# Four adjacent rows of w_v on a partition, and the columns of w_k cast into the same order

## The chip, the cores and the metric

The kernel runs on one core of a Trainium2 chip. The metric is the device time of one execution in microseconds (us). The engines are named as in the profile: PE is TensorE's matmul (PEld its weight load), DVE is VectorE, ACT is ScalarE, POOL is GpSimd, and SP is SyncE, which here only issues transfers (DMAs). "L638" is line 638 of the kernel.

## What is computed

Attention with a sliding window of 128 and 4 sink keys, over q, k, v of shape (4, 8, 768, 64), gives x of shape (4, 768, 512). Behind it comes a channel mix:

```python
x_prev = concatenate([zeros((B, 1, D)), x[:, :-1, :]], axis=1)
xk = mu_k * x + (1.0 - mu_k) * x_prev
xr = mu_r * x + (1.0 - mu_r) * x_prev
k = maximum(xk @ w_k, 0.0)                 # w_k: 512 x 1024
v = k * k @ w_v                            # w_v: 1024 x 512
r = 1.0 / (1.0 + exp(-(xr @ w_r)))         # w_r: 512 x 512
return r * v
```

The 1024 columns of w_k are the 1024 rows of w_v: the hidden index f. A sum over f does not depend on the order in which f is taken, as long as k and w_v agree on it.

## The kernel before, in words

The work is cut into 12 units of 256 rows: 4 batches of 3 tiles. Each unit passes through four functions. `prepare` casts q, k and v to bf16 and transposes q and k. `attend` makes the scores of the heads (PE, L812), their exponentials (ACT, L884), the mask product (DVE, L898), the values (PE, L917) and the scaled x (L935 or L944). `mix` transposes x and makes xk and xr (DVE, L998 and L1009). `ffn` makes relu(xk @ w_k) in chunks of 128 hidden columns with the chunk on the partitions (PE, L1062; relu at L1072 or L1076; squares at L1085 or L1089), the gate (PE, L1101; tanh at L1107), then the product with w_v (PE, L1119, in two parts of four chunks each), and last the gated output (DVE, L1128) and its store (L1135).

**Order.** Every operation is entered with `P.op`: its engine, its cost in ns, what it reads, writes, takes and holds. The order on each engine is written out by hand in `ORDER`, and the engine of the operations that could run on several in `CHOICE`. `Plan.schedule` goes through these orders with the costs, gives out buffers of the pools, and puts filler products (`fill`, L1141) into PE's order where its own clock says that PE stands idle in the first 40 us. So a cost changes neither order nor engine, but can change which buffer of a pool an operation gets and which filler stands where.

**Weights.** `load_weight` (L486) loads them in fp32 into three buffers of one pool, `w32`, each 128 partitions x 4 x 512 numbers, 1 MB. The loads come in the order w_k first half, w_k second half, w_r, w_v first half, w_v second half, all on SP's queue. The buffers of w_k are used again for w_v, so a w_v load waits for the casts of the w_k half in its buffer. A load of w_v puts row 128c + p on partition p, for four values of c: four pieces of 2 KB a partition. A load of a w_k half takes 512 columns of row 128c + p, also four pieces of 2 KB.

**Casts.** `cast` (L626) turns a quarter of a weight to bf16, 1024 numbers a partition. The four casts of w_k are operations 79 to 82: ACT (columns 0 to 255), POOL (256 to 511), ACT (512 to 767) and DVE (768 to 1023). Those of w_v are 85 to 88: DVE, DVE, ACT, DVE; they also multiply by 0.5. PE's first `ffn` takes the hidden chunks in the order 0, 2, 1, 3, then 6, 7, then 4, 5, so that it waits for ACT's first cast, POOL's, DVE's and ACT's second in that order. The product at L1119 waits with its first part for the first two casts of w_v, and with its second part for the last two, ACT's and DVE's.

Of the kernel before, what the change touches and what calls it, by code (L numbers as in the profile page):

```python
# [11 lines left out]
AF = mybir.ActivationFunctionType  # L12
# [345 lines left out]
def kernel(  # L358
# [14 lines left out]
    nc = tc.nc  # L373
# [14 lines left out]
    P = Plan()  # L388
# [25 lines left out]
    buf = P.buf  # L414
# [5 lines left out]
    def dve(n, rate=1.04):  # L420
        return 69.0 + rate * n

    def act(n):
        return 67.0 + 0.833 * n
# [61 lines left out]
    def load_weight(what, rank):  # L486
        name, part = what[:2], what[2:]
        src = {"wk": moe_w_k, "wr": moe_w_r, "wv": moe_w_v}[name].rearrange(
            "(c p) f -> p c f", p=128)
        i = "ab".index(part) if part else 0  # L490
        if name == "wk":
            src = src[:, :, 512 * i:512 * i + 512]
        elif name == "wv":
            src = src[:, 4 * i:4 * i + 4]
        key = ("w32", name, i)
        P.op("SP", 600.0, lambda: nc.sync.dma_start(out=buf[key], in_=src), rank,
             service=2930.0, descs=660, take=[("w32", key)], writes=[(name + "32", i)])

    for i, what in enumerate(LOADS):
        if what[0] == "w":  # L500
            load_weight(what, i - 100)
        elif what == "kq0":
            load(0, "kq", -100, 0, 4)
            load(0, "kq", -99.5, 4, 8)
        else:
            load(int(what[-1]), what[:-1], i - 100)
# [7 lines left out]
    for i, src in enumerate((moe_mu_k, moe_mu_r)):  # L514
        P.op("ACT", 500.0, lambda i=i, src=src: nc.scalar.dma_start(
            out=rows8[NC * i:NC * i + NC, :], in_=src.rearrange("(c p) -> c p", p=128)), -100,
            writes=[("mu8", i)], service=40.0, descs=4)
# [98 lines left out]
    def spread_mu():  # L616
# [5 lines left out]
         hold=["mup"], reads=["mup"], writes=[("mu", 0), ("mu", 1)])  # L622
# [3 lines left out]
    def cast(out, name, i, cut, rank, writes):  # L626
        key = ("w32", name, i)
        half = name == "wv"

        def emit(by):  # L630
            if by == "ACT":
                return lambda: nc.scalar.activation(out=out, in_=buf[key][cut], func=AF.Copy,  # L632
                                                    scale=0.5 if half else 1.0)
            engine = nc.vector if by == "DVE" else nc.gpsimd
            if half:
                return lambda: nc.vector.tensor_scalar(out=out, in0=buf[key][cut], scalar1=0.5,
                                                       scalar2=None, op0=ALU.mult)
            return lambda: engine.tensor_copy(out=out, in_=buf[key][cut])  # L638

        P.op("DVE", dve(1024, 0.52), emit("DVE"), rank, port=True, hold=[key],  # L640
             alts={"DVE": (dve(1024, 0.52), emit("DVE"), True),
                   "ACT": (act(1024) + 30.0, emit("ACT"), False)} |
             ({} if half else {"POOL": (1100.0, emit("POOL"), True)}),
             reads=[(name + "32", i)], writes=writes)

    for i in range(4):
        j = i % 2
        cast(wk_sb[:, :, 256 * i:256 * i + 256], "wk", i // 2,
             (slice(None), slice(None), slice(256 * j, 256 * j + 256)), 2 + i, [("wk", i)])
    for i in range(2):  # L650
        cut = (slice(None), slice(2 * i, 2 * i + 2))
        cast(wr_sb[cut], "wr", 0, cut, 8 + i, [("wr", i)])
    for i in range(4):
        j = i % 2
        cast(wv_h[:, 2 * i:2 * i + 2, :], "wv", i // 2,
             (slice(None), slice(2 * j, 2 * j + 2)), 11 + i, [("wv", i)])
# [546 lines left out]
```

## Time and profile before

| what | value |
|---|---|
| timed runs | 167.26, 169.18 and 169.84 us, median 169.18 |
| the profiled execution's own time | 166.92 us |
| its span (first to last instruction) | 165.1 us |
| busy: PE, DVE, ACT, POOL | 155.0, 144.8, 136.9, 35.2 us |
| granted clock of PE | 1.00 |
| loads of w_k, from issue to landing (median of two) | 10.3 us |
| loads of w_v, from issue to landing (median of two) | 11.2 us |
| casts of w_k: ACT (two), POOL, DVE | 1.06 (mean), 1.47, 0.68 us |
| casts of w_v: DVE (three), ACT | 0.69 (mean), 1.06 us |

All durations come from one profiled execution. In a timeline row stand the start, the time that the group covers, the engine, the line, the operation, what it writes and reads, and how many instructions; in brackets the idle time of the engine just before, and what ended it. In the chain of waits each row is a piece of the chain that ended last: start, length, engine or transfer. Rows of groups by shape give, after the bar, the busy time in us and the mean ns of one instruction. "SPq" is the time that SP spends issuing a transfer, with the stops that a full queue makes.

### The profile page before, as it was taken

The page shows a single profiled execution, that of the slowest core. Times are in us where ns is not written, and L with a number is a line of the kernel's source. Part 1 is how long each engine was busy: PE and PEld are TensorE (multiplying, and loading weights), DVE is VectorE, ACT ScalarE, POOL GpSimd, SP SyncE. Part 2 cuts the span into 40 slices and gives each one's busy share as a digit, 9 for nine tenths or more (in the row PEclk, how much of TensorE's full clock was granted, in tenths as well). Part 3 has the DMA queues.
Part 4 walks back from the last instruction along what each step waited for, and adds up shares of the span by engine and source line. Part 5 has one row for each costly group of instructions (what it writes and reads, how often), then busy time and mean ns, then how long its engine had stood idle before and what let it go on. Part 6 is the DMA issues. An engine that isn't in the chain of part 4 may idle for free.

```text
span 165.1 us, 4735 instructions
## 1 busy us (share of the span) xinstructions
PE 155.0 (94%) x1840; PEld 102.3 (62%) x1862; DVE 144.8 (88%) x356; ACT 136.9 (83%) x249; POOL 35.2 (21%) x65
## 2 busy tenths in 40 slices
PE   7889889989999998998999999999999999999992
PEld 3446566656668676676566686575855764776541
DVE  7189999999999899999999999999889899777621
ACT  3698999988999999899989999999794898482440
POOL 2885311203621044033402412310010000000000
PEclk9999999999999999999999999999999999999999
DMA  4999989999798999999999998989995992401113
GB/s 138 252 351 354 298 230 338 382 388 312 200 321 196 180 302 252 173 196 267 176 219 172 240 126 200 227 176 125 208 208 87 233 212 78 191 4 64 64 74 117
DMA packets 74453, 34.38 MB, mean 208 GB/s; under 512 B 63800, under 2 KB 66112, under 8 KB 74432
## 3 DMA queue, kind: packets, MB, share of 16 engines
q1 hardware_dynamic: 74272, 34.02, 87.6%
q8 instruction: 14, 0.23, 0.6%
q14 instruction: 7, 0.06, 0.2%
q10 hardware_dynamic: 160, 0.07, 0.1%
HBM read 24.12 MB, written 6.29 MB: 184 GB/s over the span
## 4 chain that ended last, share of the span: by engine, by line
PE 64%; DVE 18%; DMA 10%; issue 3%; ACT 2%; SPq 1%; DVEq 0%
PE bank L1119 20%; PE bank L1062 19%; PE bank L1101 10%; DMA w<-in_moe_w_v_dram 7%; DVE e L898 6%; PE bank L917 4%; PE sc L812 4%; DMA vs<-in_v_dram 3%; DVE xr L1009 2%; DVE xk L1009 2%; DVE x L935 2%; PE bank L704 2%; PE bank L971 2%; SPq L478 1%; DVE ob L1128 1%
## 5 line engine op out<-in xcount | busy, mean ns | idle before, releaser
L1062 PE MATMUL bank<-xk,wk_sb 128*128 128x256 bf16 x384 | 50.4, 273 | 0.6 <-DVE wk_sb L638 0.4
L884 ACT ACTIVATE e<-sc 128x1024 bf16<-128x1024 f32 (+1 forms) x48 | 44.9, 965 | 1.0 <-PE sc L812 0.9
L1119 PE MATMUL bank<-wv_h,kk 128*128 128x512 bf16 x170 | 44.7, 379 | 1.1 <-ACT wv_h L632 0.4
L1062 PEld LDWEIGHTS <-wk_sb 128*128 128x128 bf16 x384 | 35.5, 98 | 9.6 <-DVE wk_sb L638 0.7
L898 DVE TENSOR_TENSOR e<-e,mask 128x1024 bf16<-128x1024 bf16 (+1 forms) x48 | 31.6, 674 | 0.0
L1072 ACT ACTIVATE rl<-bank 128x512 bf16<-128x512 f32 x38 | 22.5, 613 | 8.1 <-PE bank L1062 7.9
L1119 PEld LDWEIGHTS <-kk 128*128 128x128 bf16 x184 | 16.8, 98 | 15.2 <-issue 0.7
L1009 DVE SCALAR_TENSOR_TENSOR xr<-td,mu_all,xt 128x256 bf16<-128x256 bf16 x48 | 25.4, 540 | 0.0
L1101 PE MATMUL bank<-wr_sb,xr 128*128 128x512 bf16 x88 | 23.7, 379 | 0.4
L1009 DVE SCALAR_TENSOR_TENSOR xk<-td,mu_all,xt 128x256 bf16<-128x256 bf16 x48 | 22.5, 492 | 0.1
L1085 ACT ACTIVATE kk<-rl 128x512 bf16<-128x512 bf16 x31 | 19.4, 642 | 0.7 <-DVE rl L1076 0.6
L1128 DVE SCALAR_TENSOR_TENSOR ob<-th,bank 128x512 f32<-128x512 f32 x23 | 15.7, 682 | 4.3 <-ACT th L1107 2.1
L737 POOL CAST vb<-vs 128x512 bf16<-128x512 f32 x13 | 10.0, 775 | 41.1 <-DMA vs<-in_v_dram 41.1
L1107 ACT ACTIVATE th<-bank 128x512 f32<-128x512 f32 x24 | 14.6, 608 | 4.0 <-PE bank L1101 3.9
L917 PEld LDWEIGHTS <-e 128*128 128x128 bf16 x352 | 14.4, 97 | 4.5 <-DVE e L898 1.5
L917 PE MATMUL bank<-vb,e 128*128 128x65 bf16 x352 | 16.4, 193 | 0.7 <-DVE e L898 0.5
L935 DVE TENSOR_TENSOR x<-bank,rec 128x256 bf16<-128x256 f32 x39 | 15.8, 417 | 0.6 <-DVE rec L931 0.3
L1101 PEld LDWEIGHTS <-xr 128*128 128x128 bf16 x96 | 9.0, 98 | 8.1
L812 PE MATMUL sc<-qt,kt 64*64 64x128 bf16 (+3 forms) x496 | 12.8, 226 | 0.9 <-ACT e L884 0.5
L812 PEld LDWEIGHTS <-kt 64*64 64x64 bf16 (+1 forms) x496 | 9.0, 106 | 6.5 <-issue 4.5
L944 ACT ACTIVATE x<-bank,rec 128x64 bf16<-128x64 f32 x36 | 8.4, 324 | 4.2 <-DVE rec L931 4.1
L998 DVE TENSOR_TENSOR td<-xt 128x512 bf16<-128x512 bf16 x24 | 10.4, 441 | 0.1
(88 smaller groups left out, 174.5 us busy)
## 6 DMA issues: line engine op xcount, KB each, us to landing
vs<-in_v_dram SPq DMA_DIRECT2D x24, 256.0 KB, 5.1
out_dram<-ob SPq DMA_DIRECT2D x23, 256.0 KB, 3.2
ks<-in_k_dram SPq DMA_DIRECT2D x16, 256.0 KB, 4.7
qs<-in_q_dram SPq DMA_DIRECT2D x7, 512.0 KB, 5.8
qs<-in_q_dram SPq DMA_DIRECT2D x10, 256.0 KB, 4.3
ks<-in_k_dram SPq DMA_DIRECT2D x4, 512.0 KB, 9.6
w<-in_moe_w_k_dram SPq DMA_DIRECT2D x2, 1024.0 KB, 10.3
w<-in_moe_w_v_dram SPq DMA_DIRECT2D x2, 1024.0 KB, 11.2
```

The costliest lines, as they stand in the source:

```text
L812: nc.tensor.matmul(out=sc[keys, a, o0 + f0 - q0:o0 + f1 - q0], lhsT=lhs[rows, keys], rhs=qs[rows, f0:f1], start=u not in BIAS, stop=True, ...
L884: nc.scalar.activation(out=buf[ek][:, :, lo:], in_=buf[sck][:, :, lo:], func=AF.Exp, scale=scale)
L898: nc.vector.tensor_tensor(out=at, in0=at, in1=m, op=ALU.mult)
L917: nc.tensor.matmul(out=o[:, g, a, :], lhsT=e[:, a, e0:e0 + 128], rhs=rhs, start=(T == 0 and i == 0), stop=(i == len(blocks) - 1), skip_gro ...
L935: nc.vector.tensor_tensor(out=buf["x", u][:, :, 128 * c:128 * c + 128].rearrange("p g (a d) -> p g a d", a=2), in0=view(ok)[:, :, :, 0:D], ...
L1009: nc.vector.scalar_tensor_tensor(out=buf[key][:, c, :], in0=buf[tk][:, i, :], scalar=mu[w][:, c:c + 1], in1=xt[:, c, t0 - 1:t0 + 255], op0 ...
L1062: nc.tensor.matmul(out=ps[:, i, :], lhsT=wk_sb[:, c, 128 * f:128 * f + 128], rhs=xk[:, c, :], start=(c == 0), stop=(c == NC - 1), skip_gro ...
L1072: nc.scalar.activation(out=buf[rk], in_=buf[psk].rearrange("p (i t) -> p i t", i=2), func=AF.Relu)
L1085: nc.scalar.activation(out=buf["kk", u][:, 2 * f2:2 * f2 + 2, :], in_=buf[rk], func=AF.Square)
L1101: nc.tensor.matmul(out=buf[psk], lhsT=buf["xr", u][:, c, 128 * g:128 * g + 128], rhs=wr_sb[:, c, :], start=(c == 0), stop=(c == NC - 1))
L1119: nc.tensor.matmul(out=buf[psk], rhs=wv_h[:, f, :], lhsT=buf["kk", u][:, f, 128 * g:128 * g + 128], start=(f == 0), stop=(f == NF - 1))
L1128: P.op("DVE", dve(512), lambda psk=psk, tk=tk, bk=bk: nc.vector.scalar_tensor_tensor(out=buf[bk], in0=buf[tk], scalar=1.0, in1=buf[psk], o ...
```

## The change

The load of a w_v half now puts the four adjacent rows 512i + 4p + j (j from 0 to 3) on partition p: one piece of 8 KB a partition. Chunk c of that half then holds the rows 512i + 4q + c with q on the partitions. For the hidden index of k to agree, the casts of w_k write column 4q + j of the half to place 128j + q: each cast writes the same stretch of `wk_sb` as before, and reads two runs of 128 numbers at a step of four, 16 bytes, in place of 256 adjacent ones. The load of w_k, its buffers, and the casts of w_r and w_v are as they were.

```diff
     def load_weight(what, rank):
         name, part = what[:2], what[2:]
         src = {"wk": moe_w_k, "wr": moe_w_r, "wv": moe_w_v}[name].rearrange(
-            "(c p) f -> p c f", p=128)
+            "(i p j) f -> p i j f" if name == "wv" else "(c p) f -> p c f", p=128,
+            **({"j": 4} if name == "wv" else {}))
         i = "ab".index(part) if part else 0
         if name == "wk":
             src = src[:, :, 512 * i:512 * i + 512]
         elif name == "wv":
-            src = src[:, 4 * i:4 * i + 4]
+            src = src[:, i]
         key = ("w32", name, i)
         P.op("SP", 600.0, lambda: nc.sync.dma_start(out=buf[key], in_=src), rank,
-             service=2930.0, descs=660, take=[("w32", key)], writes=[(name + "32", i)])
+             service=2730.0 if name == "wv" else 2930.0, descs=180 if name == "wv" else 660,
+             take=[("w32", key)], writes=[(name + "32", i)])
...
+        def staged():
+            if name == "wk":
+                return buf[key].rearrange("p c (q j) -> p c j q", j=4)[cut]
+            return buf[key][cut]
+
+        if name == "wk":
+            out = out.rearrange("p c (j q) -> p c j q", j=2)
+
         def emit(by):
             if by == "ACT":
-                return lambda: nc.scalar.activation(out=out, in_=buf[key][cut], func=AF.Copy,
+                return lambda: nc.scalar.activation(out=out, in_=staged(), func=AF.Copy,
                                                     scale=0.5 if half else 1.0)
...
-            return lambda: engine.tensor_copy(out=out, in_=buf[key][cut])
-
-        P.op("DVE", dve(1024, 0.52), emit("DVE"), rank, port=True, hold=[key],
-             alts={"DVE": (dve(1024, 0.52), emit("DVE"), True),
+            return lambda: engine.tensor_copy(out=out, in_=staged())
+
+        cost = dve(1024, 1.04 if name == "wk" else 0.52)
+        P.op("DVE", cost, emit("DVE"), rank, port=True, hold=[key],
+             alts={"DVE": (cost, emit("DVE"), True),
                    "ACT": (act(1024) + 30.0, emit("ACT"), False)} |
              ({} if half else {"POOL": (1100.0, emit("POOL"), True)}),
              reads=[(name + "32", i)], writes=writes)
...
         cast(wk_sb[:, :, 256 * i:256 * i + 256], "wk", i // 2,
-             (slice(None), slice(None), slice(256 * j, 256 * j + 256)), 2 + i, [("wk", i)])
+             (slice(None), slice(None), slice(2 * j, 2 * j + 2)), 2 + i, [("wk", i)])
```

No instruction moves on any engine. Beside the changed loads and casts two things differ, both from the changed costs in the planner's clock: one filler of PE, between the transposes of the second unit's x, is a bf16 product of 512 columns in place of an fp32 product of 256; and from there on two buffers of the `rl` pool are exchanged.

More of the change, by code (lines that the diff above doesn't have):

```diff
@@ L635, in emit @@
             if half:
-                return lambda: nc.vector.tensor_scalar(out=out, in0=buf[key][cut], scalar1=0.5,
+                return lambda: nc.vector.tensor_scalar(out=out, in0=staged(), scalar1=0.5,
                                                        scalar2=None, op0=ALU.mult)
-            return lambda: engine.tensor_copy(out=out, in_=buf[key][cut])
-        P.op("DVE", dve(1024, 0.52), emit("DVE"), rank, port=True, hold=[key],
-             alts={"DVE": (dve(1024, 0.52), emit("DVE"), True),
+            return lambda: engine.tensor_copy(out=out, in_=staged())
+        cost = dve(1024, 1.04 if name == "wk" else 0.52)
+        P.op("DVE", cost, emit("DVE"), rank, port=True, hold=[key],
+             alts={"DVE": (cost, emit("DVE"), True),
                    "ACT": (act(1024) + 30.0, emit("ACT"), False)} |
```

## Prediction

> **What bounds the kernel now.** I read the page's head first, then busy time by stage, then the chain of waits, then the timeline of each engine round the moved weights. Head of the page:
>
> ```profile
> span 165.1 us, 4735 instructions
> ...
> PE 155.0 (94%) x1840; PEld 102.3 (62%) x1862; DVE 144.8 (88%) x356; ACT 136.9 (83%) x249; POOL 35.2 (21%) x65
> ...
> PEclk9999999999999999999999999999999999999999
> ```
>
> TensorE (PE) is busy 94% of the span and its clock is full everywhere, so no change of clock has to be reckoned with. The head is an average; the stages differ. Busy time in stretches, one engine a column (span, then PE, PEld, DVE, ACT, POOL; then clock, DMA share, GB/s):
>
> ```profile
> 17.00:21.00 4.00, 3.37 (x43) 2.25 (x39) 4.00 (x8) 4.00 (x6) 1.47 (x1) 1.00 1.02 262
> 21.00:25.00 4.00, 3.51 (x59) 2.69 (x57) 3.74 (x12) 3.79 (x8) 0.62 (x1) 1.00 0.90 249
> 25.00:29.00 4.00, 3.89 (x58) 2.65 (x57) 3.96 (x10) 3.85 (x8) 0.62 (x1) 1.00 1.09 339
> 29.00:33.00 4.00, 3.95 (x34) 2.58 (x36) 4.00 (x9) 3.73 (x6) 1.14 (x1) 1.00 1.06 384
> 33.00:37.00 4.00, 3.71 (x63) 2.48 (x65) 4.00 (x10) 3.48 (x5) 0.00 (x0) 1.00 1.07 389
> ...
> 50.00:57.70 7.70, 7.59 (x116) 5.35 (x116) 7.16 (x22) 7.62 (x14) 0.62 (x1) 1.00 0.99 192
> 57.70:76.00 18.30, 16.97 (x227) 12.03 (x229) 18.27 (x40) 17.38 (x31) 6.56 (x9) 1.00 1.22 238
> 76.00:161.00 85.00, 84.27 (x970) 55.54 (x984) 74.57 (x184) 67.95 (x135) 9.03 (x14) 1.00 0.78 157
> ```
>
> From 17 to 37 us VectorE (DVE) has no slack, ScalarE (ACT) little, and the DMA engines are always taken. After 57.7 us first DVE is full (18.27 of 18.30 us), then PE (84.27 of 85.00). So a lag that PE or DVE carries out of the first 40 us has little room to be made up: it should reach the end. The chain of waits (start, us, what) says where the first 40 us are decided:
>
> ```profile
> 20.95 0.61 DVE wk_sb L638
> 21.56 0.05 issue
> 21.61 0.61 PE bank L1062 x4
> ...
> 24.35 0.21 DVE x L935
> 24.56 11.50 DMA w<-in_moe_w_v_dram
> 36.06 0.02 issue
> 36.09 1.07 ACT wv_h L632
> 37.16 0.04 issue
> 37.20 1.02 PE bank L1119 x4
> ```
>
> Both things that the diff touches stand here: DVE's cast of w_k, for which PE waits, and the load of w_v's second half, 11.5 us from issue to landing, with the cast behind it and PE's product behind that.
>
> **The change part by part.** It makes the two w_v loads 128 pieces of 8 KB each instead of 512 of 2 KB, makes four casts of w_k read every fourth column (16 bytes apart) instead of adjacent ones, and leaves every queue's order alone.
>
> *The loads.* Two rows on transfers, the size of all packets and the time of the two w_v loads from issue to landing (median of the two):
>
> ```profile
> DMA packets 74453, 34.38 MB, mean 208 GB/s; under 512 B 63800, under 2 KB 66112, under 8 KB 74432
> ...
> w<-in_moe_w_v_dram SPq DMA_DIRECT2D x2, 1024.0 KB, 11.2
> ```
>
> Both halves go through the DMA engines behind a backlog, so what counts is how fast they move, not when they are issued. In the two stretches in which most of them moves (29 to 37 us) the rate is 384 and 389 GB/s, so 1.049 MB takes 2.72 us. For small pieces take 238 GB/s of the stretch 57.7:76, where most pieces are rows of 64 numbers, 256 bytes (of all packets, 63800 of 74453 are under 512 bytes): per engine (a 16th) 17.2 ns for 256 B, against 84.9 ns for 2 KB at 386 GB/s. The straight line through both is 7.5 ns a piece and 0.0378 ns a byte. One 8 KB piece is then 317 ns instead of 340, and at 8 pieces an engine a load wins 0.18 us. I take 0.2 us each, 0.4 us for the landing at 36.06 (an estimate from these rows). Bounds: nothing, and a loss as far as the 249 GB/s of stretch 21:25, the slowest of this phase (4.21 us, 1.5 us more each); I stay near the first because what a larger piece does away with can hardly slow it down.
>
> *The casts of w_k.* Their rows, with the products that read them and the issue that waits for them (start, us, engine, line):
>
> ```profile
> 17.02 1.47 POOL L638 CAST wk_sb<-w 128x1024 bf16<-128x1024 f32 x1 [1.64 <-DMA w<-in_moe_w_k_dram]
> ...
> 17.84 1.07 ACT L632 ACTIVATE wk_sb<-w 128x1024 bf16<-128x1024 f32 x1
> ...
> 18.96 2.23 PE L1062 MATMUL bank<-xk,wk_sb 128*128 128x256 bf16 x16
> ...
> 20.87 0.68 DVE L638 CAST wk_sb<-w 128x1024 bf16<-128x1024 f32 x1
> ...
> 22.46 3.55 SPq L496 DMA_DIRECT2D w<-in_moe_w_v_dram  x2
> ...
> 23.42 1.05 ACT L632 ACTIVATE wk_sb<-w 128x1024 bf16<-128x1024 f32 x1
> ```
>
> DVE. No row has its read at this stride; the nearest are a cast of adjacent elements, and work that runs at a full element a step:
>
> ```profile
> L671 DVE CAST kb<-ks 128x512 bf16<-128x512 f32 x2 | 0.8, 420 | 0.0
> ...
> L638 DVE CAST wk_sb<-w 128x1024 bf16<-128x1024 f32 x1 | 0.7, 680 | 0.0
> L718 DVE COPY qt<-bank 128x512 bf16<-128x512 bf16 x1 | 0.7, 680 | 0.0
> L1041 DVE SCALAR_TENSOR_TENSOR ob<-th,bank 128x384 f32<-128x384 f32 x1 | 0.6, 555 | 1.5 <-PE bank L1031 1.5
> ...
> L1041 DVE SCALAR_TENSOR_TENSOR ob<-th,bank 128x128 f32<-128x128 f32 x1 | 0.3, 282 | 0.0
> ```
>
> From 512 to 1024 elements the cast grows by 260 ns, 0.51 ns an element; the 384 and 128 rows differ by 273 ns, 1.07 ns an element. By these, losing the double rate costs 1024 x 0.56 ns = 0.57 us. The copy of 512 out of order (L718) takes 680 ns where the cast of 512 adjacent ones takes 420; twice the difference is 0.52 us. I put 0.54 between them. Bounds: nothing, and four times 0.51 ns an element, 1.57 us, if each 16-byte step costs what four adjacent elements did. I stay at 0.54 because DVE's one reordered copy sits there.
>
> ACT. Its casts cost 0.87 ns an element (1060 ns for 1024, 616 for 512 below), and its reordered copy of 512 costs what a plain one does:
>
> ```profile
> L980 ACT COPY xt<-bank 128x512 bf16<-128x512 bf16 x14 | 8.3, 592 | 0.8 <-PE bank L971 0.7
> L718 ACT COPY qt<-bank 128x512 bf16<-128x512 bf16 x13 | 7.7, 599 | 0.4 <-PE bank L704 0.4
> ...
> L675 ACT CAST kb<-ks 128x512 bf16<-128x512 f32 x2 | 1.2, 616 | 0.0
> ```
>
> I take nothing for ACT; the other end is twice the time per element, 0.89 us for each of two casts, whose sum a rival below works out: +1.1 us, 170.3, against 169.5 with nothing. What the rows cannot tell is whether a source in SBUF behaves as theirs, which is PSUM. The Trainium skill (SBUF — State Buffer, Door 1: The DMA port swizzle) speaks against the change here: SBUF gives full bandwidth while accesses stay within a 16-byte line, and each access to a new line pays. At this step every element is a new line for every engine, so by that rule the rival's time holds, and by the reordered copies the forecast's.
>
> POOL. Bounds nothing and twice its 1.47 us. Hidden up to 1.0 us more: its output is first read by the second four of the 16 products at 18.96, some 0.56 us in, at 19.5, and it ends at 18.49. Beyond, the excess goes into the 0.4 us for which PE stands before 21.61 anyway. The w_v issue that waits for it comes at 22.46, four microseconds later.
>
> *Followed to the end.* DVE's cast ends 0.54 late, at 22.09; PE's products and ACT's relu behind it follow, ACT's second w_k cast ends near 25.0, and the second w_v issue goes out at 25.1 instead of 24.56. That is covered: the first half is then still in the queue (the two took 11.2 in the median, the second 11.5, so the first 10.9, from 22.46 to about 33.4), and the second lands 2.7 us behind it. Without that cover the 0.54 would count in full. SP's next entries are not held up: the w_v issues now spend 3.55 us, and a quarter of the pieces needs less. Then:
>
> ```profile
> 36.09 0.69 DVE L636 TENSOR_SCALAR wv_h<-w 128x1024 bf16<-128x1024 f32 x1
> ...
> 36.70 0.69 DVE L898 TENSOR_TENSOR e<-e,mask 128x1024 bf16<-128x1024 bf16 x1
> ...
> 37.43 0.43 DVE L671 CAST kb<-ks 128x512 bf16<-128x512 f32 x1
> ...
> 38.06 0.39 PE L704 MATMUL bank<-ident,kb 128*128 128x128 bf16 x4
> ```
>
> The load lands at 35.66, ACT's cast of w_v ends at 36.7 instead of 37.15. But the product at 37.20 needs DVE's cast of w_v too. DVE reached it at 36.09 without a gap, so it now starts at 36.63 and ends at 37.32: PE starts at 37.37, 0.17 later, though the data came 0.4 earlier. DVE's kb cast, 0.13 behind its predecessor today, ends at 38.27 instead of 37.86, and PE's transpose at 38.06 goes to 38.32, 0.26 late; DVE's next products keep about 0.3. PE then has no gaps to give back. Sum: +0.3 us. The saving of the load is worth nothing, because a late DVE hides it.
>
> *The rest.* One filler of PE near 24.95 becomes shorter; PE waits there for DVE's x. Two relu buffers swap names. Both nothing.
>
> The profiled execution took 166.92 us (span 165.1 and 1.8 round it), so it would take 167.2. It lies below all three timed runs (167.26, 169.18, 169.84), so I put the step on their median: 169.18 + 0.3 = **169.5 us**.
>
> **The rivals.**
> *Strided reads are free.* For it: ACT's reordered copy. Against: DVE's. DVE then starts at 36.09, ends at 36.78, ACT at 36.7; PE starts at 36.83, 0.37 early, and kb (end 37.73) cuts that to 0.25: 168.9 us.
> *ACT reads at half rate too.* Two casts of +0.89 make ACT 1.78 late. In the four stretches from 21 to 37 it is idle 0.21, 0.15, 0.27 and 0.52; the first, before the second cast, and the last, its wait for w_v, are free to take up lag (0.73), while the middle two are waits for PE, which would be late as well. DVE, fed by ACT's evacuations, follows: 1.78 - 0.73 = +1.1, 170.3 us. For it: no row shows ACT reading SBUF at a step; against: ACT's reordered copies (599 ns) cost what plain ones do (592). The rule of the Trainium skill (SBUF — State Buffer, Door 1) quoted above is this case.
> *The 8 KB pieces are slower.* The side of a real loss, with its place at 36.06: a load at rate r takes 1.049/r, and both together cost 3.4 us more (2% of the time) once r falls to 237 GB/s (4.43 us each). At 230 GB/s: +3.7, 172.9 us. Against: 389 GB/s with smaller pieces in the same place.
> *The load isn't faster.* The change would not do what it says. PE still waits for DVE until 37.37: +0.3, the forecast's time.
>
> **How the numbers follow.** Forecast 0.60 (with or without the faster load), free reads 0.18, ACT at half rate 0.14, slow pieces 0.03; 0.05 for what I don't see, spread over both sides. The timed runs lie 2.6 us apart, more than any likely case moves. Low: lowest run less 0.25, 167.0. High: highest run plus 1.1, 170.9. About 2% (3.4 us) is what a measurement of this kernel can tell from no change. Faster by that: 0.02, from the unseen alone. Slower: 0.03 of slow pieces and 0.02 unseen, 0.05. Within: 0.93.
>
> **What would show it.** DVE's w_k cast near 1.2 us, ACT's near 1.06; w_v landing 0.4 us earlier behind its issue backlog, ACT's w_v cast over before DVE's, and PE's wait there put down to DVE. Wrong if DVE's cast stays at 0.68, ACT's passes 1.5, or PE's lag at 38 us is gone or has grown past 1 us by 60.

## The result, and the profile after

| what | before | after |
|---|---|---|
| timed runs, median (16 each) | 169.01 us | 170.79 us |
| lowest and highest | 167.21, 170.38 us | 168.6, 173.4 us |
| ratio of after to before, 95% interval | | 1.0104 [1.0059, 1.015] |
| the profiled execution's own time, its span | 166.92, 165.1 us | 169.51, 167.6 us |

The change costs 1.0%: small, inside what was called no change, but a loss. The forecast was 169.5 us, +0.3; what came is 1.78 us between the medians, and +0.3 (a ratio of 1.002) lies outside the interval. The ratios here and below leave out executions more than 1.5% above the fastest of their kernel, so they are not quite the quotients of the medians.

The busy times from the page of after, the size of its packets, and the two w_v loads from issue to landing:

```profile
PE 156.5 (93%) x1861; PEld 102.7 (61%) x1861; DVE 145.8 (87%) x356; ACT 138.5 (83%) x249; POOL 39.0 (23%) x65
...
DMA packets 73685, 34.38 MB, mean 205 GB/s; under 512 B 63800, under 2 KB 66112, under 8 KB 73408
...
w<-in_moe_w_v_dram SPq DMA_DIRECT2D x2, 1024.0 KB, 9.5
```

There are 768 packets fewer (74453 before): 1024 pieces of 2 KB have become 256 of 8 KB. The loads are quicker, and ACT and POOL are busier, by 1.6 and 3.8 us (of POOL's 3.8 its cast of w_k makes 0.66). Where the time goes is in the stretches from 17 to 37 us (columns as in the prediction):

```profile
17.00:21.00 4.00, 2.59 (x27) 1.77 (x27) 4.00 (x7) 4.00 (x6) 1.27 (x1) 1.00 0.95 216
21.00:25.00 4.00, 3.19 (x54) 2.55 (x53) 3.73 (x9) 3.61 (x6) 1.25 (x2) 1.00 0.99 273
25.00:29.00 4.00, 3.05 (x38) 1.95 (x34) 2.93 (x10) 4.00 (x7) 0.39 (x1) 1.00 1.10 346
...
33.00:37.00 4.00, 4.00 (x71) 2.97 (x70) 4.00 (x10) 3.33 (x6) 0.00 (x0) 1.00 1.03 384
```

In 25 to 29 us DVE was full before (3.96 of 4.00 us) and now stands for over 1 us; ACT, which had 0.15 us free, is full; PE falls from 3.89 to 3.05. So ACT has become the late engine of this stretch; in 17 to 25 us, ahead of it, PE's busy time is already down by 0.78 and 0.32 us. The timeline of after names the instructions:

```profile
16.15 2.13 POOL L648 CAST wk_sb<-w 128x1024 bf16<-128x1024 f32 x1 [1.50 <-DMA w<-in_moe_w_k_dram]
...
16.91 1.92 DVE L909 TENSOR_TENSOR e<-e,mask 128x1024 bf16<-128x1024 bf16 x1
...
17.51 2.05 ACT L642 ACTIVATE wk_sb<-w 128x1024 bf16<-128x1024 f32 x1
...
21.33 1.06 DVE L648 CAST wk_sb<-w 128x1024 bf16<-128x1024 f32 x1
...
24.26 2.06 ACT L642 ACTIVATE wk_sb<-w 128x1024 bf16<-128x1024 f32 x1
...
27.26 1.05 ACT L991 COPY xt<-bank 128x512 bf16<-128x512 bf16 x2
...
27.86 0.43 DVE L1009 TENSOR_TENSOR td<-xt 128x512 bf16<-128x512 bf16 x1 [1.03 <-ACT xt L991]
...
37.55 1.06 ACT L642 ACTIVATE wv_h<-w 128x1024 bf16<-128x1024 f32 x1
...
37.84 1.03 PE L1112 MATMUL bank<-wr_sb,xr 128*128 128x512 bf16 x4
...
38.70 1.03 PE L1130 MATMUL bank<-wv_h,kk 128*128 128x512 bf16 x4
```

DVE's rows at the same places before, where its `td` had no wait:

```profile
16.91 0.68 DVE L898 TENSOR_TENSOR e<-e,mask 128x1024 bf16<-128x1024 bf16 x1
17.51 1.25 DVE L1009 SCALAR_TENSOR_TENSOR xr<-td,mu_all,xt 128x256 bf16<-128x256 bf16 x1
...
26.11 0.41 DVE L998 TENSOR_TENSOR td<-xt 128x512 bf16<-128x512 bf16 x1
```

Three things are to be seen. Both casts on ACT take 2.05 us instead of 1.06, POOL's 2.13 instead of 1.47, DVE's 1.06 instead of 0.68. DVE's mask product at 16.91 takes 1.92 while POOL casts, where it took 0.68; before, it was the next one on DVE, xr, that took 1.25 beside POOL's cast, and after it takes 0.47, so the two together end 0.46 later (19.22 against 18.76). And DVE stands 1.03 us at 27.86 for an ACT copy. The bracket of the w_v cast is gone: before, ACT stood there for the load (it landed at 36.06); now it comes to it at 37.55. PE's product at 38.70 has no bracket either: it follows PE's own product of the gate (37.84) without a gap. The chain of waits of after shows what took the load's place:

```profile
16.91 1.92 DVE e L909
...
21.41 1.00 DVE wk_sb L648
...
26.22 0.60 ACT kb L682
...
27.86 0.44 DVE td L1009
...
30.74 1.69 PE bank L1073 x14
```

The chain runs through DVE's held mask product and its cast of w_k, and from there no longer through the load but through what stands on ACT right behind its second w_k cast (kb at 26.22, when the cast that began at 24.26 is over), through DVE's td, to PE's products. Before, the 11.50 us of the w_v load stood there.

### The profile page after: what moved, and what is told of

Its sections match the earlier page's. It is cut to its first block, busy times and chain, and to the rows that moved or that the text cites. A ratio compares the mean times of both kernels' runs of the same rounds, so it can differ in the third digit from the quotient of the medians.

```text
span 167.6 us, 4755 instructions
## 1 busy us (share of the span) xinstructions
PE 156.5 (93%) x1861; PEld 102.7 (61%) x1861; DVE 145.8 (87%) x356; ACT 138.5 (83%) x249; POOL 39.0 (23%) x65
## 4 chain that ended last, share of the span: by engine, by line
PE 67%; DVE 22%; DMA 3%; issue 3%; ACT 2%; SPq 1%; DVEq 0%
PE bank L1130 20%; PE bank L1073 20%; PE bank L1112 12%; DVE e L909 7%; PE bank L928 5%; PE sc L823 4%; DVE xk L1020 3%; DMA vs<-in_v_dram 3%; DVE xr L1020 3%; DVE x L946 2%; DVE td L1009 2%; PE bank L715 2%; PE bank L982 2%; SPq L478 1%; DVE ob L1139 1%
## 5 line engine op out<-in xcount | busy, mean ns | idle before, releaser
L1130 PE MATMUL bank<-wv_h,kk 128*128 128x512 bf16 x184 | 46.3, 379 | 0.0
L909 DVE TENSOR_TENSOR e<-e,mask 128x1024 bf16<-128x1024 bf16 (+1 forms) x48 | 33.1, 705 | 0.4 <-ACT e L895 0.3
L1020 DVE SCALAR_TENSOR_TENSOR xr<-td,mu_all,xt 128x256 bf16<-128x256 bf16 x48 | 24.7, 524 | 0.0
L1112 PE MATMUL bank<-wr_sb,xr 128*128 128x512 bf16 x96 | 24.2, 380 | 0.1
L748 POOL CAST vb<-vs 128x512 bf16<-128x512 f32 x13 | 10.4, 807 | 38.8 <-DMA vs<-in_v_dram 38.7
L823 PE MATMUL sc<-qt,kt 64*64 64x128 bf16 (+4 forms) x496 | 12.8, 226 | 1.0 <-ACT e L895 0.5
L682 POOL CAST qb<-qs 128x512 bf16<-128x512 f32 x8 | 6.8, 863 | 19.4 <-ACT qt L729 8.5
```

What stands on the lines that cost most here:

```text
L823: nc.tensor.matmul(out=sc[keys, a, o0 + f0 - q0:o0 + f1 - q0], lhsT=lhs[rows, keys], rhs=qs[rows, f0:f1], start=u not in BIAS, stop=True, ...
L909: nc.vector.tensor_tensor(out=at, in0=at, in1=m, op=ALU.mult)
L1020: nc.vector.scalar_tensor_tensor(out=buf[key][:, c, :], in0=buf[tk][:, i, :], scalar=mu[w][:, c:c + 1], in1=xt[:, c, t0 - 1:t0 + 255], op0 ...
L1112: nc.tensor.matmul(out=buf[psk], lhsT=buf["xr", u][:, c, 128 * g:128 * g + 128], rhs=wr_sb[:, c, :], start=(c == 0), stop=(c == NC - 1))
L1130: nc.tensor.matmul(out=buf[psk], rhs=wv_h[:, f, :], lhsT=buf["kk", u][:, f, 128 * g:128 * g + 128], start=(f == 0), stop=(f == NF - 1))
```

## The experiments

All kernels are made from the changed one and keep the costs that the planner is told, so that only the named instructions differ. The first four shared one chip and its runs of the kernel before (median 168.49 us), the last four another (168.84 us).

To compare executions that begin a little earlier or later, two places are counted from the start of ACT's first w_k cast: DVE's td behind the second cast (before: 26.11 - 17.84 = 8.27 us), and PE's product with w_v's second part (before: 37.20 - 17.84 = 19.36 us). In after these are 27.86 - 17.51 = 10.35, so 2.08 late, and 38.70 - 17.51 = 21.19, so 1.83 late. The table at the end of this section has all but run 3.

**1. The casts alone.** The loads go back to four pieces of 2 KB.

```diff
-            "(i p j) f -> p i j f" if name == "wv" else "(c p) f -> p c f", p=128,
-            **({"j": 4} if name == "wv" else {}))
+            "(c p) f -> p c f", p=128)
...
-            src = src[:, i]
+            src = src[:, 4 * i:4 * i + 4]
```

> The four casts of w_k at a step of four as in the change, w_v loaded in 2 KB pieces in the old order of rows, so that k and w_v no longer agree on the order of the hidden index (this part of the computation is changed); all else is the changed kernel's. Theory A (ACT's two casts, 2.05 us instead of 1.06, make the lag): the whole loss is here, ratio to before 1.007 to 1.013, ACT's w_k casts 2.05, DVE's 1.06, POOL's 2.1, PE's first product with the second half of w_v at 38.5 to 39.2 instead of 37.2. Theory B (the 8 KB loads change what collides on the DMA queue, and that makes the lag): within 0.3% of before. Theory C (both parts cost): half of the loss, ratio 1.004 to 1.006.

Measured: 171.35 us, ratio 1.0116 [1.0065, 1.0167]. Timeline:

```profile
17.80 2.06 ACT L641 ACTIVATE wk_sb<-w 128x1024 bf16<-128x1024 f32 x1
...
28.17 0.43 DVE L1008 TENSOR_TENSOR td<-xt 128x512 bf16<-128x512 bf16 x1 [1.01 <-ACT xt L990]
...
39.08 1.03 PE L1129 MATMUL bank<-wv_h,kk 128*128 128x512 bf16 x4
```

The casts alone give the whole loss, with the same stand of DVE for ACT.

**2. The loads alone.** The casts read and write adjacent columns again.

```diff
-            if name == "wk":
-                return buf[key].rearrange("p c (q j) -> p c j q", j=4)[cut]
             return buf[key][cut]
...
-        if name == "wk":
-            out = out.rearrange("p c (j q) -> p c j q", j=2)
...
-             (slice(None), slice(None), slice(2 * j, 2 * j + 2)), 2 + i, [("wk", i)])
+             (slice(None), slice(None), slice(256 * j, 256 * j + 256)), 2 + i, [("wk", i)])
```

> w_v loaded in 8 KB pieces as in the change, the casts of w_k adjacent as before, so that k and w_v no longer agree on the order of the hidden index (this part of the computation is changed); all else is the changed kernel's. Theory A: w_v lands 0.4 to 1.2 us earlier than at 36.06, PE's wait before the product at 37.2 shrinks by up to 0.4, where DVE's cast of w_v becomes the last to be waited for; ratio to before 0.996 to 1.000. Theory B: ratio 1.007 to 1.013. Theory C: 1.004 to 1.006.

Measured: 168.39 us, ratio 0.9992 [0.9952, 1.0033]. Timeline:

```profile
19.01 1.07 ACT L637 ACTIVATE wk_sb<-w 128x1024 bf16<-128x1024 f32 x1
...
36.48 1.06 ACT L637 ACTIVATE wv_h<-w 128x1024 bf16<-128x1024 f32 x1
...
37.63 1.03 PE L1125 MATMUL bank<-wv_h,kk 128*128 128x512 bf16 x4
```

The wait for the load is gone here too, and the time is that of before: the loads neither gain nor cost what could be measured. Theory B, by which collisions of the 8 KB loads make the lag (1.007 or more), is thereby out.

**3. Two adjacent columns a step.** The casts read each pair of adjacent columns together, and so write in turn to two places 128 numbers (256 bytes) apart.

```diff
-                return buf[key].rearrange("p c (q j) -> p c j q", j=4)[cut]
+                return buf[key].rearrange("p c (q j) -> p c q j", j=4)[cut]
...
-            out = out.rearrange("p c (j q) -> p c j q", j=2)
+            out = out.rearrange("p c (j q) -> p c q j", j=2)
...
-             (slice(None), slice(None), slice(2 * j, 2 * j + 2)), 2 + i, [("wk", i)])
+             (slice(None), slice(None), slice(None), slice(2 * j, 2 * j + 2)), 2 + i, [("wk", i)])
```

> The changed kernel, with the same numbers cast to the same places, but taken in another order: two adjacent columns after each other, then a step of 16 bytes, so that the read touches each 16-byte stretch twice in a row, and the write alternates between two runs 256 bytes apart. If a read pays for each new 16-byte stretch (the Trainium skill, SBUF — State Buffer, Door 1), ACT's casts come back to 1.1 to 1.3 us, DVE's to 0.7 to 0.8, and the time to 0.996 to 1.002 of before. If instead any order that is not adjacent costs, on the write side as well, ACT's casts stay at 2.0 or more and the ratio at 1.008 or more.

Measured: 179.53 us, ratio 1.0634 [1.0583, 1.0685]. The three kinds of cast (ns: least, median, most), then the stretches:

```profile
L642 ACT ACTIVATE wk_sb<-w x2: 4739/4748/4757, 17.7 to 28.8; 128x1024 bf16<-128x1024 f32 x2
L648 POOL CAST wk_sb<-w x1: 4785/4785/4785, 16.3 to 16.3; 128x1024 bf16<-128x1024 f32 x1
L648 DVE CAST wk_sb<-w x1: 2740/2740/2740, 23.5 to 23.5; 128x1024 bf16<-128x1024 f32 x1
```

```profile
17.00:21.00 4.00, 1.27 (x21) 0.62 (x14) 4.00 (x3) 4.00 (x3) 4.00 (x1) 0.98 1.04 231
21.00:25.00 4.00, 2.54 (x13) 1.80 (x13) 4.00 (x8) 3.66 (x4) 1.63 (x2) 0.50 1.00 297
```

This missed badly: the casts became more than twice as slow as the ones they should have cured. Two things differ from the changed kernel's casts at once: each number is written 256 bytes from the one before it, and the innermost run is two numbers long where it was 128. Which of the two costs so much was not tried. PE then starved (busy 1.27 of 4.00 us), and its granted clock was 0.50 in the stretch behind that, so the ratio may hold more than the casts' price. As a test of the read side the run tells nothing; the next one does.

**4. Two rows on a partition.** Pieces of 4 KB, and casts with a step of two numbers, 8 bytes.

```diff
-            **({"j": 4} if name == "wv" else {}))
+            **({"j": 2} if name == "wv" else {}))
...
-            src = src[:, i]
+            src = src[:, 2 * i:2 * i + 2]
...
-        P.op("SP", 600.0, lambda: nc.sync.dma_start(out=buf[key], in_=src), rank,
+        P.op("SP", 600.0, lambda: nc.sync.dma_start(
+            out=buf[key].rearrange("p (i j) f -> p i j f", j=2) if name == "wv" else buf[key],
+            in_=src), rank,
...
-                return buf[key].rearrange("p c (q j) -> p c j q", j=4)[cut]
+                return buf[key][cut].rearrange("p c (q j) -> p c j q", j=2)
...
-             (slice(None), slice(None), slice(2 * j, 2 * j + 2)), 2 + i, [("wk", i)])
+             (slice(None), slice(None), slice(256 * j, 256 * j + 256)), 2 + i, [("wk", i)])
```

> Two adjacent rows of w_v on a partition in place of four: pieces of 4 KB, and the casts of w_k read at a step of two, 8 bytes. If a read pays for each new 16-byte stretch, two reads fall on each: ACT's casts near 1.06 us, DVE's 0.68 to 0.8, ratio to before 0.996 to 1.001. If every step other than one costs alike, ACT's casts are near 2.05 and the ratio is 1.008 to 1.012. If the price grows with the step in bytes, ACT's casts lie near 1.5 and the ratio near 1.004.

Measured: 168.67 us, ratio 0.9978 [0.9919, 1.0037]. The casts, then the timeline:

```profile
L644 ACT ACTIVATE wk_sb<-w x2: 1144/1152/1161, 17.8 to 23.6; 128x1024 bf16<-128x1024 f32 x2
L650 POOL CAST wk_sb<-w x1: 1111/1111/1111, 16.9 to 16.9; 128x1024 bf16<-128x1024 f32 x1
L650 DVE CAST wk_sb<-w x1: 681/681/681, 21.0 to 21.0; 128x1024 bf16<-128x1024 f32 x1
```

```profile
17.83 1.16 ACT L644 ACTIVATE wk_sb<-w 128x1024 bf16<-128x1024 f32 x1
...
36.00 1.06 ACT L644 ACTIVATE wv_h<-w 128x1024 bf16<-128x1024 f32 x1 [0.27 <-DMA w<-in_moe_w_v_dram]
37.11 1.02 PE L1132 MATMUL bank<-wv_h,kk 128*128 128x512 bf16 x4 [0.18 <-ACT wv_h L644]
```

At 8 bytes a step the casts cost within 0.1 us of the adjacent ones on every engine; at 16 bytes ACT and POOL take about twice as long. ACT waits for the load again here, 0.27 us. The Trainium skill (SBUF — State Buffer, Door 1: The DMA port swizzle) says that two accesses to each 16-byte line are needed for full speed; the trace agrees on the reads: with two a line 1.15 us on ACT, with one 2.05. A step of 12 bytes, which would tell a price for each new line from one for any step above 8 bytes, was not tried.

**5. ACT's casts adjacent, POOL's and DVE's at a step.** A tuple names the quarters that are read at a step; here 1 and 3, in the next three runs (0, 1, 3), (3,) and (0, 2).

```diff
+        step4 = name == "wk" and rank - 2 in (1, 3)
+
         def staged():
-            if name == "wk":
+            if step4:
                 return buf[key].rearrange("p c (q j) -> p c j q", j=4)[cut]
...
-        if name == "wk":
+        if step4:
             out = out.rearrange("p c (j q) -> p c j q", j=2)
...
-             (slice(None), slice(None), slice(2 * j, 2 * j + 2)), 2 + i, [("wk", i)])
+             (slice(None), slice(None), slice(2 * j, 2 * j + 2) if i in (1, 3)
+              else slice(256 * j, 256 * j + 256)), 2 + i, [("wk", i)])
```

> The changed kernel (8 KB loads), but ACT's two casts of w_k read and write adjacent columns as before; POOL's and DVE's still read every fourth. The hidden orders of w_k and w_v then disagree, so the output is not the reference's. ACT casts back to 1.06 us, DVE 1.06, POOL about 2.1. Theory 'ACT's casts carry the loss': DVE is 0.85 us late at 22 us as in the changed kernel, but no longer 2.1 late at 28 us, and under 0.8 late at 50 us; ratio 1.001 to 1.004. Rival 'DVE is the bound of this stage, and POOL's and DVE's casts carry it': still over 1.2 us late at 50 us; ratio 1.008 to 1.011.

Measured: 169.31 us, ratio 1.0025 [0.9976, 1.0075]. Timeline:

```profile
16.58 2.09 POOL L650 CAST wk_sb<-w 128x1024 bf16<-128x1024 f32 x1 [1.55 <-DMA w<-in_moe_w_k_dram]
...
17.29 1.92 DVE L912 TENSOR_TENSOR e<-e,mask 128x1024 bf16<-128x1024 bf16 x1
...
17.81 1.07 ACT L644 ACTIVATE wk_sb<-w 128x1024 bf16<-128x1024 f32 x1
...
27.25 0.43 DVE L1012 TENSOR_TENSOR td<-xt 128x512 bf16<-128x512 bf16 x1
...
38.09 1.03 PE L1133 MATMUL bank<-wv_h,kk 128*128 128x512 bf16 x4
```

The ratio is in the range of "ACT's casts carry the loss", and DVE's stand for ACT at td is gone. But DVE is still 1.17 us late there: POOL's and DVE's casts hold this stage up by themselves. How much of that is left at the end, the interval doesn't tell. By plain start times DVE is 1.13 us late at 50 us, between the bounds of the two theories; it began 0.38 late, at 16 us, before any of these casts mattered.

**6. Only ACT's second cast adjacent.**

> The changed kernel, but of the four casts of w_k only ACT's second one, at 24.3 us, reads adjacent columns; the other three read every fourth. The hidden orders disagree, so the output is not the reference's. Theory 'the second ACT cast is the one that matters, DVE stands 1.03 us for ACT's copy behind it': DVE's stand at 27.9 us is under 0.2, its lag at 28 us about 1.1 instead of 2.1, ratio 1.004 to 1.006. Rival 'ACT's first cast, through the products behind it, costs as much or more': the lag at 28 us stays over 1.6, ratio 1.008 or more.

Measured: 169.83 us, ratio 1.0035 [0.9985, 1.0086]. Timeline:

```profile
17.18 2.06 ACT L644 ACTIVATE wk_sb<-w 128x1024 bf16<-128x1024 f32 x1
...
27.11 0.43 DVE L1012 TENSOR_TENSOR td<-xt 128x512 bf16<-128x512 bf16 x1
...
37.95 1.03 PE L1133 MATMUL bank<-wv_h,kk 128*128 128x512 bf16 x4
```

The wait at td is gone, as the theory of the second cast has it, but counted from ACT's first cast td comes 1.66 late: 0.42 less than with all four at a step. ACT's first cast, too, is worth 0.49 (1.66 against the 1.17 of run 5). Neither of the two is "the one". The 1.66 is the rival's (over 1.6), but the ratio lies below both forecasts, and its interval reaches into both.

**7. Only DVE's cast at a step**: the prediction's own case.

> The changed kernel, but only DVE's cast of w_k reads every fourth column; ACT's two and POOL's read adjacent ones. The hidden orders disagree, so the output is not the reference's. This is the prediction's own case, in which ACT and POOL cost nothing. DVE cast 1.06 us, ACT 1.06, POOL 1.04 to 1.47. By the forecast's steps, with its DVE term at the 0.38 us measured instead of 0.54: DVE 0.38 late at 22 us, 0.1 to 0.3 us at the end, ratio 1.0005 to 1.002. Rival 'a lag of DVE in this stage grows on its way to the end, whatever it comes from': over 0.8 us late at the end, ratio 1.005 or more.

Measured: 168.69 us, ratio 0.9965 [0.9914, 1.0016]. Timeline:

```profile
16.56 1.10 POOL L650 CAST wk_sb<-w 128x1024 bf16<-128x1024 f32 x1 [1.54 <-DMA w<-in_moe_w_k_dram]
...
17.29 0.92 DVE L912 TENSOR_TENSOR e<-e,mask 128x1024 bf16<-128x1024 bf16 x1
...
17.94 1.07 ACT L644 ACTIVATE wk_sb<-w 128x1024 bf16<-128x1024 f32 x1
...
26.24 0.43 DVE L1012 TENSOR_TENSOR td<-xt 128x512 bf16<-128x512 bf16 x1
...
36.83 1.02 PE L1133 MATMUL bank<-wv_h,kk 128*128 128x512 bf16 x4
```

No loss: td comes 0.03 late and PE's product 0.47 early. The rival by which a lag of DVE grows to 0.8 us is out for this cast. But the 0.03 is not all that a slower cast on DVE costs: counted from ACT's first cast, DVE came to this one 0.26 sooner than before (20.71 - 17.94 = 2.77 us, against 20.87 - 17.84 = 3.03), and so was 0.12 late behind it instead of 0.38. Against run 5, which differs from this one in POOL's cast alone, td comes 1.14 sooner: so POOL's cast at a step, 2.09 instead of 1.10 us, makes nearly all of run 5's 1.17.

**8. Only ACT's two casts at a step.**

> The changed kernel, but only ACT's two casts of w_k read every fourth column; POOL's and DVE's read adjacent ones. The hidden orders disagree, so the output is not the reference's. ACT casts 2.05 us each, DVE 0.68, POOL 1.04 to 1.47. Theory 'ACT's casts carry the loss': DVE on time until 21 us, then over 1.2 us late at 28 us, 0.7 to 1.2 at 50 us, ratio 1.006 to 1.009. Rival 'POOL's and DVE's casts carry it': under 0.4 late at 50 us, ratio 1.000 to 1.003.

Measured: 170.31 us, ratio 1.01 [1.001, 1.019]. Timeline:

```profile
17.81 2.05 ACT L644 ACTIVATE wk_sb<-w 128x1024 bf16<-128x1024 f32 x1
...
27.65 0.43 DVE L1012 TENSOR_TENSOR td<-xt 128x512 bf16<-128x512 bf16 x1 [1.15 <-ACT xt L994]
...
38.49 1.03 PE L1133 MATMUL bank<-wv_h,kk 128*128 128x512 bf16 x4
```

ACT's casts alone bring the wait at td and a loss about that of the whole change, a little above the range expected (and DVE 1.37 late at 50 us, where 0.7 to 1.2 was expected). The rival, by which POOL's and DVE's casts would carry it, wanted DVE under 0.4 late at 50 us, and the 1.37 speaks against it. Its ratio, under 1.003, is only at the edge of this interval, the widest of the eight.

All together (us late against before, counted from the start of ACT's first cast):

| kernel | at a step of 16 bytes | DVE's td | PE's product | ratio, 95% interval |
|---|---|---|---|---|
| after | all four | 2.08 | 1.83 | 1.0104 [1.0059, 1.015] |
| 1 | all four, old loads | 2.10 | 1.92 | 1.0116 [1.0065, 1.0167] |
| 8 | ACT's two | 1.57 | 1.32 | 1.01 [1.001, 1.019] |
| 6 | ACT's first, POOL's, DVE's | 1.66 | 1.41 | 1.0035 [0.9985, 1.0086] |
| 5 | POOL's, DVE's | 1.17 | 0.92 | 1.0025 [0.9976, 1.0075] |
| 7 | DVE's | 0.03 | -0.47 | 0.9965 [0.9914, 1.0016] |
| 4 | none (8 bytes) | 0.16 | -0.08 | 0.9978 [0.9919, 1.0037] |
| 2 | none, new loads | -0.14 | -0.74 | 0.9992 [0.9952, 1.0033] |

The lags are of single executions, and how long DVE is held by POOL depends on when POOL's cast begins: 0.82 us ahead of ACT's first in before, 1.23 to 1.38 in after and runs 1 and 5 to 8, 1.10 in run 2 and 0.97 in run 4. Lags that differ by a few tenths should not be ranked.

ACT's casts alone make 1.57 us at td and POOL's and DVE's 1.17, but all four only 2.08: the two overlap. In run 5, where DVE is late and ACT quick, ACT stands 0.44 and 0.93 us for PE ahead of its second cast; in after, where ACT's first cast takes 0.99 longer, it stands only 0.39. No version is faster than before beyond its interval; runs 4 and 7 come nearest. Run 2, whose start was 1.17 us late, shows that the earlier product is not by itself a shorter time.

## Why the prediction was right and wrong

The time lies in its range, and no change by 2% was right. Its account was not. The time is 0.11 us under the upper end, which had been set by a rival's 1.1 us and not by the forecast's 0.3: the time is inside thanks to the room made for that rival, not for the forecast's own reason. The prediction named its own tests: wrong if ACT's cast passes 1.5 us (it takes 2.05), or if the lag has grown past 1 us by 60 (PE's product at 38.70 stands 1.50 behind its 37.20 already).

*The step that failed: "I take nothing for ACT".* The reordered copies showed ACT unharmed by an order, but their source is PSUM, as the prediction itself said; a source in SBUF at this step costs 0.99 us more for each of two casts. This is the rival "ACT reads at half rate too", which had 0.14. Its bound of 0.89 each was near. Its working, twice the excess less the 0.73 us that ACT has free, gives 1.25 with the 0.99 measured; run 8, ACT alone, is 1.32 late at PE's product, and the rest up to 1.83 comes with POOL's and DVE's casts. The reordered copies were the wrong neighbour: they differ from these casts in the memory, in the type (bf16) and in the order, and which of these spared them was not tried. The rule of the 16-byte line in the Trainium skill (SBUF — State Buffer, Door 1), which the prediction had set beside this rival, agrees with ACT's 2.05 us.

*POOL's cast: the cover was named for the wrong engine.* "Hidden up to 1.0 us" looked at PE, which reads the result, and at SP. PE never waited for POOL's result. But DVE works beside POOL, and is held while POOL casts; and PE stands 0.99 us at 19.62 for DVE's xk, which comes behind the held product, where it had no wait before. In after POOL ends at 16.15 + 2.13 = 18.28 and DVE's mask product at 16.91 + 1.92 = 18.83, 0.55 us later, of the 0.68 that it takes undisturbed; in run 7 POOL ends at 17.66 and the product at 18.21, again 0.55 later. So the product does nearly all its work after POOL is done, and each us on POOL costs DVE one: 1.92 against 0.92 us, with POOL at 2.13 against 1.10. In the kernel before, DVE's mask product came first, at 16.91, and POOL at 17.02 waited: its 1.47 us was no pure duration, for without the step of 16 bytes it takes 1.04 to 1.11 in runs 2, 4, 7 and 8. By the Trainium skill (SBUF — State Buffer, SBUF: two separate sides) the pair of ports that POOL and DVE share is locked for a whole instruction, by whichever starts first; the traces agree, with 0.54 to 0.56 us in after and in runs 1, 2 and 4 to 8. In run 3 they don't: the product ended 0.08 us before POOL's cast of 4.79, and why stays open.

*DVE's cast.* Taken as 0.54, measured 0.38 (0.68 to 1.06): the step was right and its size 0.16 too large. What followed from it, +0.3 at the end, was not seen: run 7 shows no loss, helped by the 0.26 us named there.

*The loads.* 0.2 us each agrees with the traces. The two w_v loads of after, issue times and us to landing:

```profile
L497 SPq DMA_DIRECT2D w<-in_moe_w_v_dram x2: 340/1156/1972, 22.0 to 26.3; - x2
...
DMA to landing us min/median/max: 8.6/9.5/10.4
```

The first lands at 22.0 + 10.4 = 32.4, the second at 26.3 + 8.6 = 34.9, 2.5 behind it, where it was 2.7. The same difference is 2.5 in runs 2 and 5 to 8, and 2.8 in run 1 with its pieces of 2 KB. The second was issued 1.8 us later than before, behind ACT's late cast, and still landed 1.1 earlier: the cover that the prediction gave this delay, a queue that is still full, held for three times the lag that it reckoned with. The load's gain is worth nothing, as forecast, but for another reason: ACT comes to the data 2.6 us after it lands, and PE, full from 33 to 37 us, comes to its product later still. The wait of PE for DVE's cast of w_v (37.37) did not happen: in after and in runs 1, 2 and 5 to 8 PE's product follows its own product of the gate without a gap. In run 7, the case that these steps were made for, it starts at 36.83, by chance the very time that the rival of free reads had worked out.

*Carried to the end.* That a lag out of the first 40 us is not made up fits the kernel after: 1.83 late at PE's product, and 1.78 us between the medians. The profiled span of after is 2.5 us longer; the 0.7 over that is not accounted for and lies within what single executions differ by (its own kernel's runs lie 4.8 us apart).

*What stays open.* How the loss divides between ACT's two casts, and how much of the 1.17 us of run 5 reaches the end: the intervals are some 1% wide. And of run 3, whether the written side or the short innermost run is to blame, and what it would cost without the fall of the clock.

## What to carry to other kernels

Before you move an order from a transfer into a cast, price the cast on every engine that runs a part of it, from a row with the same memory, type and step as its source; here reordered copies from PSUM did not tell what casts from SBUF would pay. In fp32, keep a step of reads at 8 bytes: two rows on a partition cost nothing that could be measured here (and gained nothing either), four doubled the casts on ACT and POOL. And where POOL gets slower, look first at what DVE does beside it, not at who reads POOL's result.

## What the runs showed of the hardware

- Casts of 1024 fp32 numbers a partition in SBUF to bf16, read adjacent, at 8 and at 16 bytes a step: ACT 1.06, 1.15, 2.05 us; POOL 1.04 to 1.10, 1.11, 2.09 to 2.13; DVE 0.68, 0.68, 1.06.
- The same casts with pairs of adjacent numbers read and each pair written to two places 256 bytes apart: ACT 4.75, POOL 4.79, DVE 2.74 us. That is over twice the casts at 16 bytes a step on each engine; the jumps of the writes and the short innermost run were not told apart.
- A mask product on DVE, 0.68 us alone, ends 0.54 to 0.56 us after the cast of w_k on POOL that began ahead of it, however long that takes (1.04 to 2.13 us, eight traces). With a cast of 4.79 us (run 3) it ended 0.08 before.
- 1 MB into 128 partitions landed 2.5 us behind the one ahead of it in pieces of 8 KB (six traces), 2.7 and 2.8 in pieces of 2 KB (before and run 1).
